# A fused attention, channel-mix and channel-FFN kernel: the planner's ranks from a table, and one temporary in another buffer

## The chip, the cores and the metric

The kernel runs on one core of one Trainium2 chip. The metric is the time of one execution in microseconds of device time (us); lower is better. A core has five engines with an instruction stream each: TensorE (PE, matmuls; PEld are its weight loads), VectorE (DVE), ScalarE (ACT), GpSimd (POOL) and SyncE (SP, which here only issues DMAs). TensorE's clock has two levels, 1.2 and 2.4 GHz; the profile gives the granted share of the full one as PEclk.

## The reference

Three stages follow each other; batch 4, sequence 576, model width 512.

```python
# stage 1: attention, 8 heads of 64; causal window of 32 (heads 0-3), or every 4th of 128 (heads 4-7)
scores = np.where(masks[None], scale * np.matmul(q, k.transpose(0, 1, 3, 2)), -1e9)
attn = np.exp(scores - scores.max(-1, keepdims=True))
x = np.matmul(attn / (attn.sum(-1, keepdims=True) + 1e-9), v)          # -> (4, 576, 512)
# stage 2: channel mix
x_prev = np.concatenate([np.zeros((B, 1, D)), x[:, :-1, :]], axis=1)
xk = mu_k * x + (1.0 - mu_k) * x_prev
xr = mu_r * x + (1.0 - mu_r) * x_prev
k = np.maximum(xk @ w_k, 0.0)                                          # 512 -> 1024
y = 1.0 / (1.0 + np.exp(-(xr @ w_r))) * (k * k @ w_v)                  # r * v
# stage 3: low-rank token mix, then a two-layer FFN over channels
h = y.transpose(0, 2, 1) @ U @ V                                       # rank 32 over the 576 positions
u = y + h.transpose(0, 2, 1)
out = u + np.maximum(u @ w_ch1, 0.0) @ w_ch2                           # 512 -> 2048 -> 512
```

## The kernel before, in words

**The work on TensorE.** The large products run in float32 precision as three matmuls on a high and a low part of each operand: L1006, L1007, L1008 (128x288) in the channel mix, whose positions are cut into 8 chunks of 288 (two for each batch); L1283, L1284, L1285 (128x256) in the FFN's first layer (`ch1`); L1370, L1371, L1372 (128x256) in its second (`ch2`). The FFN's matrix products are saved by a seven-product scheme on 2x2 blocks, so sums and differences of blocks (`ws`, `s`, `tt`, `hb`, `hc`, `ha`) are made on DVE and their high and low parts (`wh`, `wl`, `boxw`, `boxraw`, `boxA`, `boxB`, `boxx`) on ACT, DVE and POOL.

**Between the two.** In the last two chunks of the channel mix the low-rank token mix of batches 0 to 2 runs beside it, that of batch 3 in the FFN's first steps. For each batch: DVE forms `y` = r times v from a PSUM bank (L1100); SP stores it to `ytmp` in DRAM (L1102), and loads a whole batch back as `yb` (L1123, `load_y`, 1152 KB); PE transposes it in five blocks (L1132, `y_tr`), multiplies by U (L1150, `u_mm`, accumulated over the five) and, once ACT and DVE have taken the sum as `g` (L432), by V (L1167, `v_mm`, eight matmuls a batch); DVE adds `yb` (L1175, `us`); SP stores that to `uf` (L1179), from which blocks `ub` of 256 positions come back (L1207) as the FFN's input. `yb` has two buffers. PE executes in the order written, so a `y_tr` whose `yb` has not landed holds up every product behind it.

**What sets the order.** Nothing is issued while the kernel's functions run: each calls `op()`, which appends one of 3453 operations to a list with its engine, an assumed duration and the tiles it reads and writes. `plan()` then orders them. Its `forward(rank)` walks time: for each engine it looks at the operations within WINDOW = 160 of the oldest one not done, sorted by rank (on SP they stay in program order), takes the first that can start, and takes a later one only if that could start more than 100 ns sooner. `backward` works out from such a walk how late each operation may start, plus a bias by kind (EARLIER) and by place (BIAS); a mixture of these over 16 passes is the next rank, first for the first chunks (CUTS), then for the whole. The walk with the earliest end is kept. Where the walk sees PE wait over 600 ns for a PSUM bank's next user (`fill`, L262), it puts matmuls on a tile of zeros ahead of it (L1616, `psS<-zero`, 128x512). The order is then fixed in each engine's instruction stream: on the chip every engine takes its own in turn and waits by semaphore.

**Buffers of the change.** `x_sum(g, name, a, b)` (L1228) makes a difference of two `ub` blocks of group g in a temporary `tt`, which `loose(tag, n, name)` (L568) puts in a slot that another tile used before. Tag "y" has one slot, that of the channel mix's last `y` tiles; tag "m" has one slot, that of the channel mix's mixing temporaries. The FFN runs over five groups of positions, g = 0 to 4; group 0's first step begins while the channel mix ends.

Of the kernel before, what the change touches and what calls it, by code (L numbers as in the profile page):

```python
# [16 lines left out]
B, H, S, D = 4, 8, 576, 64  # L17
DM, DFF, DCH, RANK = 512, 1024, 2048, 32
P = 128
HS = S // 2  # L20
NCH = 2 * B
# [44 lines left out]
BIAS = (-20.0, -20.0, -20.0)  # L66
# [24 lines left out]
PLAN_PRINT = None  # L91
PASSES = 16
CUTS = ((1, 3), (4, 8))
DAMP = 0.8
# [3 lines left out]
EARLIER = {"d": -20, "k2": -10, "wx": -5, "cl": 5}  # L98
# [5 lines left out]
CODE_NS, CODE_BUSY, CODE_GO = 5000.0, 6500.0, 1300.0  # L104


@with_exitstack
def tile_attention_mix_channel(
# [20 lines left out]
    ops, cuts = [], {}  # L129
    bias = 0.0  # L130
# [21 lines left out]
    def op(eng, ns, fn, r=(), w=(), more=100, lock=False, mode=None, size=0):  # L152

        o = Op()
        o.eng, o.ns, o.fn, o.r, o.w, o.more, o.lock, o.mode, o.size = eng, ns, fn, list(r), list(w), more, lock, mode, size
        o.bias = bias
        ops.append(o)

    def plan():
# [30 lines left out]
        def x_end(x):  # L190
            if x.end is not None:
                return x.end
            end = 0.0
            for u in reversed(x.ops):
                if u.i >= upto:
                    continue
                if u.done is None:
                    return NEVER
                end = max(end, u.done)
            x.end = end  # L200
            return end
# [20 lines left out]
        upto = len(ops)  # L222

        def forward(rank):
# [5 lines left out]
            free = dict.fromkeys(("PE", "DVE", "ACT", "POOL", "SP"), 0.0)  # L230
            held = {"DVE": 0.0, "POOL": 0.0}
            queues = {e: [o for o in ops[:upto] if o.eng == e] for e in free}
# [3 lines left out]
            order = []  # L236
# [36 lines left out]
            while len(order) < upto:  # L273
                while ops[low].done is not None:
                    low += 1
                best = None
                for e, q in queues.items():
                    pick = None
                    near = []
# [4 lines left out]
                    if rank and e != "SP":  # L284
                        near.sort(key=lambda o: rank.get(o.i, o.i * 1e6))
                    for o in near:
                        t = ready(o)
                        if t is None:
                            continue
                        t = max(t, free[e])  # L290
                        if o.lock:
                            t = max(t, held["POOL" if e == "DVE" else "DVE"])
                        if o.mode and mode[e] != o.mode:
                            t += 90 if e == "PE" else 1283
                        key = t
# [7 lines left out]
                    if pick and (best is None or pick[0] < best[0]):  # L303
                        best = pick
# [26 lines left out]
            return max(o.done for o in order if o.eng == "PE"), order  # L331

        users = [[] for _ in ops]
        for o in ops:
            for d in o.deps:
                users[d.i].append(o)
            for x in o.first:
                if x.at >= x.bufs:
                    for u in x.line[x.at - x.bufs].ops:
                        if u is not o:  # L340
                            users[u.i].append(o)

        def backward(end, order):

            late = {}
            for o in reversed(order):
                t = end
                for u in users[o.i]:
                    if u.i < upto:
                        t = min(t, late.get(u.i, end) - 40 - (o.done - o.at - o.ns))  # L350
                late[o.i] = t - o.ns
            return {o.i: late[o.i] + 1000.0 * (EARLIER.get(o.kind, 0) + o.bias) for o in order}

        rank = {}
        keep = 0
        for keep_to, upto in [tuple(cuts.get(c, len(ops)) for c in x) for x in CUTS] + [(len(ops), len(ops))]:
            fixed, end = {i: x for i, x in rank.items() if i < keep}, None
            keep = keep_to
            for n in range(PASSES):
                used = dict(rank)  # L360
                got = forward(rank)
                if end is None or got[0] < end:
                    end, best = got[0], used
                    order = [(o, o.at, o.done, o.before) for o in got[1]]
                new = backward(got[0], got[1])
                rank = {i: fixed[i] if i in fixed else DAMP * rank[i] + (1 - DAMP) * x if i in rank else x for i, x in new.items()}
            rank = best if len(best) == upto else rank
            if PLAN_PRINT:
                print("planned to", upto, round(end))
        for o, o.at, o.done, o.before in order:  # L370
            pass
        order = [x[0] for x in order]
# [195 lines left out]
    def loose(tag, n, name):  # L568
        return Part(Lazy([P, n * Q], F32, tag, name, LOOSE[tag]), 0, n * Q)
# [658 lines left out]
    def x_sum(g, name, a, b):  # L1228
        x_slot(g, name)
        t = tt[g, name] = loose("y", 2, "tt")  # L1230
        part_sum(t, a, b, ALU.subtract)
        part_split(T_ENG, t, *operands[g, name])
# [293 lines left out]
    for t in range(NPAIR):  # L1526
        begin(LOADS[t])
        units += fresh(1)
        bias = BIAS[0]
        steps(units[-1:], 2)  # L1530
        bias = 0.0
    for t in range(NPAIR):
        convert_to(t + 1, 1)
        bias = BIAS[1]
        steps(units[t : t + 1], 4)
        mix(0, t, "r")
        bias = BIAS[2]
        first[t]()
        bias = 0.0
# [7 lines left out]
    for c in range(NCH - 1):  # L1547
        cuts[c] = len(ops)
# [28 lines left out]
    cuts[NCH] = len(ops)  # L1577
# [133 lines left out]
```

## Time and profile before

| | |
|---|---|
| time, median of 3 runs | 733.75 us (732.14, 733.75, 734.02) |
| time of the profiled execution | 731.21 us |
| its span, first to last instruction | 729.3 us |
| PE busy | 715.1 us, 98% of the span |
| PE weight loads | 690.8 us, 95% |
| DVE busy | 603.3 us, 83% |
| ACT busy | 420.6 us, 58% |
| POOL busy | 165.2 us, 23% |
| mean granted TensorE clock | 0.995 of full |

The table comes from the page of the profile and from the list of runs. A share of busy time is an average over the whole span: attention and the channel mix to about 345 us, the FFN from there to the end. What an engine waits for in one stretch is read from the waits and the timeline of that stretch. A row of a timeline gives the start and the duration of an instruction; as matmuls are pipelined, the distance from one start to the next is what one costs on PE.

### The profile page before, as it was taken

What the parts mean: (1) busy time and instruction counts of PE and PEld (TensorE: products, weight loads), DVE (VectorE), ACT (ScalarE), POOL (GpSimd) and SP (SyncE); (2) the same over time, 40 slices, a digit from 0 to 9 for tenths busy, and PEclk for the clock granted to TensorE, in tenths of its full rate; (3) what the DMA queues carried; (4) which work ended last, traced back from release to release, by engine and by line L of the source; (5) the groups of instructions that cost most, each with busy time, mean ns of one, the idle gap of its engine ahead of it and who ended that gap; (6) DMA issues with size and microseconds to landing.
All of it is one profiled execution on the core that took longest, in us unless ns stands there. A gap on an engine that the chain in (4) does not pass through costs nothing.

```text
span 729.3 us, 19236 instructions
## 1 busy us (share of the span) xinstructions
PE 715.1 (98%) x7527; PEld 690.8 (95%) x7527; DVE 603.3 (83%) x1500; ACT 420.6 (58%) x1049; POOL 165.2 (23%) x189
## 2 busy tenths in 40 slices
PE   8999999999999999899999999999999999999997
PEld 6778999999999999799899999999999999999997
DVE  5979997889677736599998898999999999797935
ACT  5997867667785837175653543455475545454421
POOL 0101464546463634031200111010000101010100
PEclk9999999999999999999999999999999999999999
DMA  8986268587647520826634456433554111304204
GB/s 314 363 293 216 67 200 284 186 284 250 214 160 255 185 76 26 284 93 204 206 113 169 147 179 208 147 124 116 153 179 131 59 45 56 105 15 133 74 14 130
DMA packets 69963, 117.71 MB, mean 161 GB/s; under 512 B 6128, under 2 KB 41200, under 8 KB 69872
## 3 DMA queue, kind: packets, MB, share of 16 engines
q1 hardware_dynamic: 69872, 116.49, 48.3%
q8 instruction: 59, 0.97, 0.6%
q14 instruction: 32, 0.26, 0.1%
HBM read 85.00 MB, written 31.46 MB: 160 GB/s over the span
## 4 chain that ended last, share of the span: by engine, by line
PE 65%; DVE 17%; issue 7%; DMA 5%; ACT 4%; POOL 1%; SPq 0%; DVEq 0%; POOLq 0%; ACTq 0%
PE psM L1006 7%; PE psM L1008 6%; PE psM L1007 6%; PE psM L1283 6%; PE psM L1285 6%; PE psM L1284 6%; PE psM L1034 4%; PE psS L1372 3%; PE psS L1370 3%; PE psS L1371 3%; PE psM L1370 3%; PE psM L1372 3%; PE psM L1371 3%; DMA w2f<-w 2%; PE psS L923 2%
## 5 line engine op out<-in xcount | busy, mean ns | idle before, releaser
L1006 PE MATMUL psM<-xk,wh 128*128 128x288 f32 x336 | 101.9, 303 | 0.1
L1007 PE MATMUL psM<-xk,wl 128*128 128x288 f32 x336 | 99.5, 296 | 0.0
L1008 PE MATMUL psM<-xk,wh 128*128 128x288 f32 x336 | 99.3, 296 | 0.0
L1006 PE MATMUL psM<-k2s,wh 128*128 128x288 f32 x224 | 67.1, 300 | 0.0
L1007 PE MATMUL psM<-k2s,wl 128*128 128x288 f32 x224 | 66.0, 295 | 0.0
L1008 PE MATMUL psM<-k2s,wh 128*128 128x288 f32 x224 | 65.9, 294 | 0.0
L1006 PEld LDWEIGHTS psM<-xk,wh 128*128 128x128 f32 x336 | 63.6, 189 | 1.2 <-DVE k L1082 0.3
L1007 PEld LDWEIGHTS psM<-xk,wl 128*128 128x128 f32 x336 | 63.7, 189 | 0.2
L1008 PEld LDWEIGHTS psM<-xk,wh 128*128 128x128 f32 x336 | 63.6, 189 | 0.0
L430 POOL TENSOR_TENSOR boxw<-ub,boxw 128x512 fp32r<-128x512 f32 x13 | 19.2, 1475 | 191.7 <-ACT boxw L435 147.8
L430 POOL TENSOR_TENSOR k2s<-k,k2s 128x288 fp32r<-128x288 f32 x49 | 44.3, 908 | 61.8 <-ACT k2s L435 60.6
L1283 PE MATMUL psM<-boxraw,wh 128*128 128x256 f32 x198 | 56.0, 283 | 0.7 <-ACT hc L1353 0.5
L1285 PE MATMUL psM<-boxraw,wh 128*128 128x256 f32 x198 | 55.2, 279 | 0.0
L1284 PE MATMUL psM<-boxraw,wl 128*128 128x256 f32 x198 | 55.1, 279 | 0.0
L1283 PE MATMUL psM<-boxw,wh 128*128 128x256 f32 x186 | 53.6, 288 | 1.3 <-ACT hc L1353 0.7
L1372 PE MATMUL psS<-boxx,wh 128*128 128x256 f32 x192 | 54.3, 283 | 0.0
L1284 PE MATMUL psM<-boxw,wl 128*128 128x256 f32 x186 | 52.3, 281 | 0.0
L1285 PE MATMUL psM<-boxw,wh 128*128 128x256 f32 x186 | 52.2, 281 | 0.0
L722 ACT ACTIVATE pr<-pr,mn 128x64 f32<-128x64 f32 x144 | 48.0, 337 | 6.3 <-DVE mn L713 6.2
L430 POOL TENSOR_TENSOR xk<-m,xk 128x288 fp32r<-128x288 f32 x48 | 42.3, 892 | 34.6 <-ACT xk L435 25.1
L430 POOL TENSOR_TENSOR boxraw<-ub,boxraw 128x512 fp32r<-128x512 f32 x12 | 17.9, 1496 | 125.6 <-ACT boxraw L435 89.2
L435 ACT ACTIVATE boxx<-ha 128x512 fp32r<-128x512 f32 x32 | 20.1, 627 | 41.4 <-DVE ha L591 29.2
(235 smaller groups left out, 2576.8 us busy)
## 6 DMA issues: line engine op xcount, KB each, us to landing
w<-w2raw SPq DMA_DIRECT2D x32, 512.0 KB, 5.3
w<-w1raw SPq DMA_DIRECT2D x20, 512.0 KB, 6.1
w2f<-w SPq DMA_DIRECT2D x32, 256.0 KB, 2.6
ub<-uf SPq DMA_DIRECT2D x32, 256.0 KB, 3.4
ws<-w2f SPq DMA_DIRECT2D x24, 256.0 KB, 3.6
raw<-qk SPq DMA_DIRECT2D x16, 320.0 KB, 6.4
ytmp<-y SPq DMA_DIRECT2D x32, 144.0 KB, 1.9
yb<-ytmp SPq DMA_DIRECT2D x4, 1152.0 KB, 7.1
```

Source lines behind the costliest of these rows:

```text
L430: op("POOL", t, lambda: nc.gpsimd.tensor_tensor(out=out_(), in0=a(), in1=b(), op=ALU.subtract), r, w, 40, lock=True)
L722: nc.scalar.activation(pr[:, d : d + KW], pr[:, d : d + KW], AF.Exp, bias=mn[:, i : i + 1], scale=-1.0, accum_out=sm[:, i : i + 1])
L1006: nc.tensor.matmul(a, lhsT=wh, rhs=xh, start=start, stop=False)
L1007: nc.tensor.matmul(a, lhsT=wl, rhs=xh, start=False, stop=False)
L1008: nc.tensor.matmul(a, lhsT=wh, rhs=xl, start=False, stop=stop)
L1034: pe(2, MM1, lambda o=o, acc=accs[o]: nc.tensor.matmul(acc()[:, :HS], lhsT=whole_w[w]()[:, o * P : (o + 1) * P], rhs=cols(src, n), start=f ...
L1283: nc.tensor.matmul(a, lhsT=wh(*wi), rhs=xh(*ci), start=start and n == 1, stop=False, skip_group_check=True)
L1284: nc.tensor.matmul(a, lhsT=wl(*wi), rhs=xh(*ci), start=False, stop=False, skip_group_check=True)
L1285: nc.tensor.matmul(a, lhsT=wh(*wi), rhs=xl(*ci), start=False, stop=last, skip_group_check=True)
L1370: nc.tensor.matmul(a, lhsT=wh(*wi), rhs=xh(), start=start, stop=False, skip_group_check=True)
L1371: nc.tensor.matmul(a, lhsT=wl(*wi), rhs=xh(), start=False, stop=False, skip_group_check=True)
L1372: nc.tensor.matmul(a, lhsT=wh(*wi), rhs=xl(), start=False, stop=stop, skip_group_check=True)
```

## The change

The ranks no longer come from the passes of `forward` and `backward`: `backward`, the passes and all their constants (BIAS, EARLIER, CUTS, DAMP, PASSES) are gone, and `forward` runs once on `RANKS`, 3453 numbers in steps of 50 ns that are unpacked from a string. The table was found beforehand by a search over shifted ranks, with the mean of five perturbed planner executions as its measure. `forward`, with its windows, assumed durations and fills, is the same; SP's operations still stand in program order among themselves as candidates. In `x_sum`, group 0's `tt` takes the slot of tag "m" and no longer that of "y". The functions of the body are otherwise as before, 54 lines lower; the fill is L1663 and the sorting by rank includes every operation of the list.

```diff
-PASSES = 16
-CUTS = ((1, 3), (4, 8))
-DAMP = 0.8
 NORM_ENG = ("DVE", "DVE", "ACT", "DVE", "POOL")
...
-EARLIER = {"d": -20, "k2": -10, "wx": -5, "cl": 5}
...
+RANKED = (
+    'c-k%73EWrH)(7y@{G`%|kfcExNlJxO<|xs<#t4;^A<8u+xkVx&QOI<OLeivr6^WFRN^^<OK&cd(R66f>y}Lf2)Bc}*)?UMJt-bd6OemUV!#!D{EPLu;p'
...
+)
+RANKS = [50 * x for x in itertools.accumulate(struct.unpack("<3453i", zlib.decompress(base64.b85decode(RANKED))))]
...
-                    if rank and e != "SP":
-                        near.sort(key=lambda o: rank.get(o.i, o.i * 1e6))
+                    if e != "SP":
+                        near.sort(key=lambda o: rank[o.i])
...
-        def backward(end, order):
...
-            return {o.i: late[o.i] + 1000.0 * (EARLIER.get(o.kind, 0) + o.bias) for o in order}
...
-        for keep_to, upto in [tuple(cuts.get(c, len(ops)) for c in x) for x in CUTS] + [(len(ops), len(ops))]:
...
+        order = forward(RANKS)
...
     def x_sum(g, name, a, b):
         x_slot(g, name)
-        t = tt[g, name] = loose("y", 2, "tt")
+        t = tt[g, name] = loose("y" if g else "m", 2, "tt")
         part_sum(t, a, b, ALU.subtract)
         part_split(T_ENG, t, *operands[g, name])
```

Each engine has the same operations as before. Their place in its stream differs for 767 of PE's 945 operations (by 4.6 places in the mean, 35 at most), 905 of DVE's 1175, 503 of ACT's 773, 71 of POOL's 185 and 161 of SP's 375. One fill is new; the others have the sizes they had. Three places follow.

**SP, around the load of batch 1.** `ytmp<-y` stores a tile of the channel mix, `ws<-w2f` loads a block of the second layer's weights, `w2f<-w` stores one, `yb<-ytmp_67` is the load of batch 1. Before:

```order
L1102 DMA ytmp_69<-y 128x288
L621 DMA ws<-w2f_71 128x512
L621 DMA ws<-w2f_70 128x512
L1102 DMA ytmp_69<-y 128x288
L1123 DMA yb<-ytmp_67 128x4x576
L511 DMA w2f_84<-w_4799 128x512
```

and after the change:

```order
L1156 DMA ytmp_69<-y 128x288
L1177 DMA yb<-ytmp_67 128x4x576
L675 DMA ws<-w2f_71 128x512
L675 DMA ws<-w2f_70 128x512
L565 DMA w2f_84<-w_4802 128x512
```

The load of batch 1 has moved up past two loads of weights and one store of `y`. On PE the transposes of batch 1 stand behind 480 products of three matmuls (128x288), where they stood behind 484: twelve matmuls earlier.

**PE, ahead of the transposes of batch 3.** `psS<-vs,g` are the `v_mm` of batch 2; `boxw`, `wh` and `wl` are operands of the FFN's first layer. Before:

```order
L1283 MATMUL psM<-boxw_5407,wh 128x256
L1284 MATMUL psM<-boxw_5407,wl 128x256
L1285 MATMUL psM<-boxw_5407,wh 128x256
L1167 MATMUL psS<-vs,g 128x288 x8
L1283 MATMUL psM<-boxw_5340,wh 128x256
L1284 MATMUL psM<-boxw_5340,wl 128x256
L1285 MATMUL psM<-boxw_5340,wh 128x256
```

(the transposes follow nine matmuls later), and after:

```order
L1337 MATMUL psM<-boxw_5391,wh 128x256
L1338 MATMUL psM<-boxw_5391,wl 128x256
L1339 MATMUL psM<-boxw_5391,wh 128x256
L1221 MATMUL psS<-vs,g 128x288 x4
L1663 MATMUL psS<-zero 128x512 x2
L1186 MATMUL psS<-cst_t,yb 128x128 x4
```

The eight `v_mm` of batch 2 are now in two halves with twelve first-layer matmuls between them (the second half is in the rows), and a fill of two matmuls stands ahead of the transposes of batch 3. In all, 3 `u_mm`, 36 first-layer matmuls and 8 `v_mm` stood between the channel mix's last matmul and those transposes; now 3, 48, 8 and the fill do. From the last `u_mm` to the first `v_mm` there were 12 first-layer matmuls; now there are 24. On SP the load of batch 3 stays behind the last two stores of `y` and one load of `ub`; two more loads of `ub` now stand ahead of those stores. On DVE `tt` of group 0 and the `boxw` made from it stood behind the last `y`; now they stand ahead of the last two.

**PE, the first and second layer's interleaving in an early FFN step.** `boxB,boxA` belong to the second layer, `boxraw` and `boxw` to the first. Before:

```order
L1283 MATMUL psM<-boxw_5340,wh 128x256
L1284 MATMUL psM<-boxw_5340,wl 128x256
L1285 MATMUL psM<-boxw_5340,wh 128x256
L1283 MATMUL psM<-boxraw,wh 128x256
L1284 MATMUL psM<-boxraw,wl 128x256
L1285 MATMUL psM<-boxraw,wh 128x256
```

and after:

```order
L1338 MATMUL psM<-boxw_5345,wl 128x256
L1339 MATMUL psM<-boxw_5345,wh 128x256
L1424 MATMUL psM<-boxB 128x256
L1425 MATMUL psM<-boxB 128x256
L1426 MATMUL psM<-boxB 128x256
L1424 MATMUL psM<-boxB,boxA 128x256
L1425 MATMUL psM<-boxB 128x256
L1426 MATMUL psM<-boxB,boxA 128x256
L1337 MATMUL psM<-boxraw,wh 128x256
```

Six matmuls of the second layer now stand between the product of `boxw` and that of `boxraw`; before, the two followed each other directly. The same six are put between the corresponding products of a later step.

## Rows read from the trace of the kernel before

**Rows 1.** The page: busy us of each engine, share of the span.

```profile
PE 715.1 (98%) x7527; PEld 690.8 (95%) x7527; DVE 603.3 (83%) x1500; ACT 420.6 (58%) x1049; POOL 165.2 (23%) x189
```

**Rows 2.** Waits of PE, whole span: total us, times, longest us.

```profile
PE psS L1132 <- DMA yb<-ytmp: 3.6, 1, 3.6
...
PE psM L1283 <- DVE hb L1333: 0.8, 2, 0.6
```

**Rows 3.** Timeline of PE around the transposes of batch 1.

```profile
299.54 0.29 PE L1008 MATMUL psM<-xk,wh 128*128 128x288 f32 x1
303.40 1.09 PE L1132 MATMUL psS<-cst_t,yb 128*128 128x128 f32 x4 [3.56 <-DMA yb<-ytmp]
...
306.92 0.40 PE L1150 MATMUL psS<-yh,us 128*128 128x512 f32 x1
```

**Rows 4.** Timeline of PE at transposes of batch 0 that did not wait.

```profile
267.01 0.29 PE L1008 MATMUL psM<-xk,wh 128*128 128x288 f32 x1
267.14 0.60 PE L1132 MATMUL psS<-cst_t,yb 128*128 128x128 f32 x4
267.57 0.60 PE L905 MATMUL psS<-cst_t,pr 128*128 128x128 f32 x4
```

**Rows 5.** Windows: PE, PEld, DVE, ACT, POOL busy, PEclk, DMA share, GB/s.

```profile
299.80:303.40 3.60, 0.04 (x2) 0.03 (x1) 0.97 (x3) 0.00 (x0) 0.00 (x0) 0.97 0.98 357
303.40:306.00 2.60, 2.60 (x12) 2.60 (x13) 0.69 (x1) 0.60 (x1) 0.00 (x0) 0.50 0.73 216
```

**Rows 6.** Timeline of SP around the load of batch 1.

```profile
290.46 0.88 SPq L621 DMA_DIRECT2D ws<-w2f  x2
...
292.56 0.53 SPq L1123 DMA_DIRECT2D yb<-ytmp  x1
```

**Rows 7.** DMA issues of 284 to 304 us: KB each, median us to landing.

```profile
yb<-ytmp SPq DMA_DIRECT2D x1, 1152.0 KB, 10.7
...
ytmp<-y SPq DMA_DIRECT2D x4, 144.0 KB, 4.2
ws<-w2f SPq DMA_DIRECT2D x2, 256.0 KB, 3.9
```

**Rows 8.** The tile yb, its four loads, us to landing.

```profile
DMA to landing us min/median/max: 5.9/7.1/10.7
```

**Rows 9.** DMA issues of 348 to 350 us, columns as in rows 7.

```profile
yb<-ytmp SPq DMA_DIRECT2D x1, 1152.0 KB, 5.9
```

**Rows 10.** Timeline of PE, end of the channel mix to batch 3.

```profile
344.82 0.40 PE L1150 MATMUL psS<-yh,us 128*128 128x512 f32 x1
...
345.29 0.28 PE L1283 MATMUL psM<-boxw,wh 128*128 128x256 f32 x1
...
346.70 0.40 PE L1150 MATMUL psS<-yh,us 128*128 128x512 f32 x1
...
349.86 0.80 PE L1167 MATMUL psS<-vs,g 128*128 128x288 f32 x4 [1.34 <-DVE g L432]
...
354.87 0.60 PE L1132 MATMUL psS<-cst_t,yb 128*128 128x128 f32 x4
```

**Rows 11.** Timelines of DVE and SP: the last y, the load of batch 3.

```profile
346.37 0.45 DVE L1100 TENSOR_TENSOR y<-psM,sg 128x288 f32<-128x288 f32 x1
...
349.84 0.69 DVE L591 TENSOR_TENSOR tt<-ub 128x512 f32<-128x512 f32 x1
...
348.70 0.53 SPq L1123 DMA_DIRECT2D yb<-ytmp  x1
```

**Rows 12.** Windows, columns as in rows 5, up to batch 3.

```profile
340.00:350.00 10.00, 8.65 (x66) 8.14 (x65) 9.88 (x21) 5.62 (x11) 0.96 (x1) 1.00 0.40 131
350.00:355.00 5.00, 4.59 (x22) 4.08 (x23) 4.97 (x12) 1.15 (x2) 1.28 (x1) 0.66 1.00 342
```

**Rows 13.** Timeline of PE, an early FFN step and a later one.

```profile
386.38 0.38 PE L1283 MATMUL psM<-boxraw,wh 128*128 128x256 f32 x1 [0.53 <-ACT hc L1353]
...
467.51 0.39 PE L1283 MATMUL psM<-boxw,wh 128*128 128x256 f32 x1 [0.65 <-ACT hc L1353]
```

More of the change, by code (lines that the diff above doesn't have):

```diff
@@ L1 @@
+import base64
+import itertools
+import struct
+import zlib
 from contextlib import ExitStack
@@ L65 @@
 SC_M = 4
-BIAS = (-20.0, -20.0, -20.0)
 LOADS = ("q0 c m w q1", "q2 v1 q3 v0 w", "v2 w", "w w v3 w w w", "")
@@ L126, in f32 @@
         return ap.bitcast(F32)
-    ops, cuts = [], {}
-    bias = 0.0
+    ops = []
     class Lazy:
@@ L155, in op @@
         o.eng, o.ns, o.fn, o.r, o.w, o.more, o.lock, o.mode, o.size = eng, ns, fn, list(r), list(w), more, lock, mode, size
-        o.bias = bias
         ops.append(o)
@@ L194, in x_end @@
             for u in reversed(x.ops):
-                if u.i >= upto:
-                    continue
                 if u.done is None:
@@ L220, in ready @@
             return t
-        upto = len(ops)
         def forward(rank):
@@ L231, in forward @@
             held = {"DVE": 0.0, "POOL": 0.0}
-            queues = {e: [o for o in ops[:upto] if o.eng == e] for e in free}
+            queues = {e: [o for o in ops if o.eng == e] for e in free}
             mode = {"PE": None, "ACT": "exp"}
@@ L272, in fill @@
                 return None, 0, 0
-            while len(order) < upto:
+            while len(order) < len(ops):
                 while ops[low].done is not None:
@@ L330, in forward @@
                 order.append(o)
[L331 to L341, printed above, removed]
-        def backward(end, order):
[L345 to L351, printed above, removed]
-            return {o.i: late[o.i] + 1000.0 * (EARLIER.get(o.kind, 0) + o.bias) for o in order}
-        rank = {}
-        keep = 0
-        for keep_to, upto in [tuple(cuts.get(c, len(ops)) for c in x) for x in CUTS] + [(len(ops), len(ops))]:
[L357 to L372, printed above, removed]
+            return order
+        order = forward(RANKS)
         if PLAN_PRINT:
@@ L1528, in tile_attention_mix_channel @@
         units += fresh(1)
-        bias = BIAS[0]
         steps(units[-1:], 2)
-        bias = 0.0
     for t in range(NPAIR):
         convert_to(t + 1, 1)
-        bias = BIAS[1]
         steps(units[t : t + 1], 4)
         mix(0, t, "r")
-        bias = BIAS[2]
         first[t]()
-        bias = 0.0
     convert_to(NPAIR + 1, 1)
@@ L1547, in tile_attention_mix_channel @@
     for c in range(NCH - 1):
-        cuts[c] = len(ops)
         cur = quanta(c) if c else first
@@ L1576, in tile_attention_mix_channel @@
             prep(*what)
-    cuts[NCH] = len(ops)
     convert_to(len(jobs))
```

94 lines of the change are left out of this document (added).

## The prediction

> **What bounds the kernel now.** I read the page first, then PE's list of waits, then the timelines of the places that the list names, then the windows of clock and DVE there. PE is busy for 715.1 us of a span of 729.3 [rows 1], so all that any order can win is the 14 us in which it is not, and some slow-clock time. DVE with 83% is idle too often to bound the whole, but not in every stretch. The list of waits [rows 2] is short: one wait of 3.6 us for a `yb` load, and then single waits of 1.3 us and less. So three places can pay, and I price each by the distance between starts, which holds slow-clock time as well as idle time.
>
> Place A, the transposes of batch 1: from L1008's start at 299.54 to L1150's at 306.92 [rows 3] PE takes 7.38 us for 13 matmuls of 128x288 and four transposes. At full speed a 128x288 matmul takes 0.13 us (267.01 to 267.14) and four transposes 0.43 (267.14 to 267.57) [rows 4], together 13 x 0.133 + 0.43 = 2.16. So 5.2 us are lost there: about 3.7 in the wait, and 1.5 after it because the granted clock stood at 0.50, the 1.2 GHz level, for the 2.6 us that followed it [rows 5].
>
> Place B, from the channel mix's last matmul to the transposes of batch 3: 344.82 to 354.87 is 10.05 us [rows 10] for 3 `u_mm` at 0.235 (two from 344.82 to 345.29), 36 first-layer matmuls at 0.118 (twelve in the 1.41 us from 345.29 to 346.70) and 8 `v_mm` at 0.133: 0.7 + 4.2 + 1.1 = 6.0. So 4.05 are lost: 1.34 waiting for `g`, the rest in a shorter wait behind it and to a clock that averaged 0.66 from 350 to 355 [rows 12]. DVE is full there, 14.85 of 15 us from 340 to 355 [rows 12]. The batch 3 transposes themselves did not wait: the load was issued at 348.70 [rows 11], 2.3 us after the start of the last `y` at 346.37, and took 5.9 [rows 9], which makes 354.6, just before PE came at 354.87.
>
> Place C: two first-layer products wait 0.53 and 0.65 us for ACT to read their bank into `hc` [rows 13].
>
> **The change part by part.** No operation goes; the work on each engine is the same, so only waits and clock can change.
>
> A. The load of batch 1 now stands where the two `ws` loads were issued, at 290.46 in place of 292.56 [rows 6]: 2.1 us earlier. PE comes to its transposes twelve matmuls earlier, at 299.7 - 1.6 = about 298.1. What decides is how long the load takes. It took 10.7 us, the longest of four; the shortest took 5.9, and the median is 7.1 [rows 8]. From 290.46 these make 301.2 (10.7), 296.4 (5.9) and 297.6 (7.1). I take 7.1: the 656 KB that went out just ahead of it (two `ws` of 256 and a `ytmp` of 144, [rows 7]) are now behind it, and the load of batch 3, with two `ytmp` and one `ub` ahead, took 5.9 [rows 9]; but the 656 KB still run beside it. Then PE does not stop, the clock stays up, and all 5.2 us come back. Bounds: -0.6 (10.7 again: PE still waits from 298.1 to 301.2, 3.1 us, and the 1.5 of clock stay: 5.2 - 3.1 - 1.5 = 0.6) and -5.2. The `ws` loads and the store that now come behind are 2 us later; the first `ws` consumers are the DVE sums of the FFN's weights, ahead of which DVE had half its time free (0.97 of 3.6 us busy, [rows 5]).
>
> The rows leave open how far the load runs beside its neighbours: the `ws` loads of this stretch took 3.9 us and the `ytmp` stores 4.2 in the median [rows 7], and 357 GB/s were moved while PE waited [rows 5]. If only what is ahead of it counted, it would land at 292.56 + 10.7 = 303.3 less the 1.9 us that 656 KB take at 357 GB/s, so at 301.4: 3.3 us of wait left, a gain of 0.4 in place of 5.2. The Trainium skill (DMA: Bandwidth & Descriptors, "Queues, rings and completion order") speaks for this: SP owns one ring on each DMA engine, and an engine consumes its descriptors in ring order, so a transfer issued later would not take bandwidth from one issued earlier. By that rule A would be -0.4 and the time 733.1 in place of 728.3. I keep it as R1; the 5.9 of batch 3 [rows 9] says that a load with little ahead is quick, and at 290.46 less is ahead than at 292.56.
>
> B. Twelve more first-layer matmuls (1.4 us) fit ahead of the transposes of batch 3, and the wait for `g` gets 24 matmuls of cover (2.8 us) where it had 12: its 1.34 us go, and the shorter one with it, for the second half of the `v_mm` stands behind twelve more. But the chain `y`, store, load that ends in `yb` stays: PE comes after 0.7 + 48 x 0.118 + 1.1 = 7.4, with the fill (two matmuls of 512 columns at 0.23) 7.9 us, and the load, if it lands as late after the last channel-mix matmul as before, at 10.0. So a wait of about 2 us for `yb` takes the place of that for `g`, and the clock falls after it as it did at A, up to 1.5 us. The interval remains 10.05 us long, holds 1.4 us more work, and pays up to 1.5 behind it: zero. Bounds: -1.5 (the clock stays up) and +1.5 (two more `ub` loads of 256 KB stand ahead in SP's queue, 512 KB at 357 GB/s = 1.5 us later).
>
> The moved buffer belongs here: in slot "m" `tt` need not wait until the last `y` tiles are stored, and its matmuls are half of the new cover. On DVE it and its `boxw`, 1.4 us as two instructions of 0.7 (`tt` took 0.69 [rows 11]), now come ahead of the last two `y`. I cost that at nothing, because other DVE work for the weights moves behind the `y` in exchange; without that, on a full DVE, the last `y` and with it the load are 1.4 us later, which the bound of +1.5 covers.
>
> C. Six second-layer matmuls, 6 x 0.118 = 0.71 us, now lie between the products at both places: more than 0.53 and 0.65, so both waits go: -1.2 (bounds -1.2 and 0). The two waits for `hb` [rows 2] have the same matmuls ahead as before and stay.
>
> D. The rest of the new order. 767 of PE's operations have moved, and each step of the FFN could meet a wait of the size that such waits have now, about half a microsecond (0.53 and 0.65 [rows 13], 0.8 in two [rows 2]). I take two of 0.5, +1.0 (bounds 0 and +2.5, five of them).
>
> Sum: 731.2 (the profiled execution) - 5.2 + 0 - 1.2 + 1.0 = 725.8. That execution was 2.5 us below the median of its three runs, 733.75, so on the footing of the median the forecast is 725.8 + 2.5 = **728.3 us**, 0.7% less. About 0.3%, 2.2 us, is what a measurement of this kernel can tell from no change: faster is below 731.5, slower above 736.0.
>
> **The rivals.**
>
> R1, the load of batch 1 lands late all the same. For it: 357 GB/s were moving while PE waited [rows 5], so bytes may be what the load waits for, and the weights that stood ahead still share the DMA engines when they are behind. By the Trainium skill's rule on ring order (DMA: Bandwidth & Descriptors, same section) it is this rival that comes true. Against it: half of the four loads took 7.1 us or less. A gives 0.4 to 0.6, so 731.2 - 0.6 - 1.2 + 1.0 + 2.5 = 732.9, or 733.1: within 0.3%.
>
> R2, DVE gives back at B what A wins. For it: DVE has 14.85 of 15 us filled up to 355 [rows 12], so if it was behind by its own work and not by PE's, the last `y` comes no earlier, and PE, 5.2 us ahead, waits for `yb` as much longer. Against it: DVE was free for much of 299.8 to 306 [rows 5], so the work that follows PE moves forward with it. Then 731.2 - 1.2 + 1.0 + 2.5 = 733.5: no change.
>
> R3, slower: the first- and second-layer steps stall in the new order. Two waits for ACT's read into `hc` now hold PE up, at 0.59 us each [rows 13]. The place is the FFN from 355 us on, the mechanism that a product reaches its bank before ACT has read it. From the forecast to 736.0 it takes 7.7 us, 13 such waits; with 14 of them the time is 736.6. For it: the order is fixed by assumed durations, and two waits show that these are off by half a microsecond in places. Against it: the changed order puts six matmuls where the two worst were.
>
> **How the numbers follow.** The forecast has a chance of 0.60, R1 0.12, R2 0.16, R3 0.12. The forecast is all faster, R1 and R2 lie within 0.3% (a small part of R1 with a good B is faster), R3 is slower: faster 0.61, same 0.27, slower 0.12. The range: its lower end is the best case, A -5.2, B -1.5, C -1.2, D 0, 723.3 on the profiled execution's footing and 725.8 on the median's; I set 724.5 between them. The upper end is to hold R1 and most of R2: 733.6. The likeliest case alone would have 725 to 731.
>
> **What would show it.** In the changed kernel's trace: the load of batch 1 issued near 290.5 and landing by 298, with no wait of PE for `yb` at its transposes and the clock at the 2.4 GHz level through 300 to 306 (A); a wait for `yb` of about 2 us at batch 3, none for `g`, and a stretch at 1.2 GHz behind it (B); no wait for `hc` at the two places of rows 13 (C); the list of waits otherwise with a few entries of half a microsecond (D). The prediction is wrong if `yb` still holds PE up at batch 1 for 3 us (R1), if the wait at batch 3 grows to 5 us and more (R2), or if the list of waits shows a dozen waits for `hc` or `hb` in the FFN (R3).

## The result: 725.3 us in place of 731.9, and the profile after

The changed kernel takes **725.26 us**, the median of 6 executions (723.6 to 726.49); the kernel before, on the same chips, 731.93 (6 executions, 730.68 to 734.02). The ratio is 0.9904, 95% interval 0.9882 to 0.9925: faster by about 1%. The forecast was a ratio of 728.3 / 733.75 = 0.9926, just above the upper end of that interval. In microseconds it was 3.0 too high; 1.8 of that is the baseline, whose three runs then known had a median of 733.75, where all six have 731.93. The profiled execution took 726.0 us (span 724.2), where the forecast on that footing was 725.8.

The page, busy us of each engine, answers to [rows 1]: PE is busy for as long within 1 us, and the span is 5.1 us shorter, so most of what went is time in which PE stood.

```profile
PE 714.3 (99%) x7529; PEld 689.3 (95%) x7529; DVE 593.0 (82%) x1500; ACT 424.1 (59%) x1049; POOL 164.5 (23%) x189
```

Waits of PE in the changed kernel, columns as in [rows 2]:

```profile
PE psM L1337 <- DVE hb L1387: 1.2, 2, 0.6
PE psS L1186 <- DMA yb<-ytmp: 0.9, 1, 0.9
PE psS L1663 <- DVE us L1229: 0.5, 1, 0.5
...
PE psS L1221 <- DVE g L486: 0.4, 2, 0.2
...
PE psM L1337 <- ACT hp L1362: 0.4, 1, 0.4
```

The 3.6 us for `yb` are gone, and so is `hc`; `g` is down from 1.3 to 0.4 in two waits. The two for `hb` have grown from 0.8 [rows 2] to 1.2. A wait of 0.9 for `yb` is new, and it is that of batch 3.

**Place A in the changed kernel.** SP issues the load of batch 1 ahead of the `ws` loads; the DMA issues of 290 to 290.6 us (KB, us to landing) give 6.0 us for it, and PE's timeline runs through the transposes:

```profile
290.15 0.53 SPq L1177 DMA_DIRECT2D yb<-ytmp  x1
290.78 1.04 SPq L675 DMA_DIRECT2D ws<-w2f  x2
```

```profile
yb<-ytmp SPq DMA_DIRECT2D x1, 1152.0 KB, 6.0
```

```profile
297.62 0.60 PE L1186 MATMUL psS<-cst_t,yb 128*128 128x128 f32 x4
297.97 0.38 PE L1060 MATMUL psM<-xk,wh 128*128 128x288 f32 x1
```

The load landed at 290.15 + 6.0 = 296.15 and PE came 1.5 us later, with no wait in brackets. The windows (columns as in [rows 5]) show the clock at its full level where it had been at 0.50:

```profile
299.80:303.40 3.60, 3.60 (x29) 3.34 (x28) 3.49 (x9) 0.93 (x2) 0.00 (x0) 1.00 0.82 282
303.40:306.00 2.60, 2.60 (x21) 2.51 (x20) 1.46 (x4) 0.16 (x1) 0.00 (x0) 1.00 0.61 185
```

**Place B in the changed kernel**, PE from the end of the channel mix (339.86 is the `u_mm` that stood at 344.82 in [rows 10]) to the transposes of batch 3 and what follows them:

```profile
339.86 0.40 PE L1204 MATMUL psS<-yh,us 128*128 128x512 f32 x1
...
345.15 0.80 PE L1221 MATMUL psS<-vs,g 128*128 128x288 f32 x4 [0.24 <-DVE g L486]
...
347.50 1.50 PE L1221 MATMUL psS<-vs,g 128*128 128x288 f32 x4
...
349.52 0.73 PE L1663 MATMUL psS<-zero 128*128 128x512 f32 x2 [0.53 <-DVE us L1229]
351.20 1.11 PE L1186 MATMUL psS<-cst_t,yb 128*128 128x128 f32 x4 [0.94 <-DMA yb<-ytmp]
352.68 0.58 PE L1337 MATMUL psM<-boxw,wh 128*128 128x256 f32 x1 [0.37 <-ACT hp L1362]
...
355.20 0.41 PE L1339 MATMUL psM<-boxw,wh 128*128 128x256 f32 x1
```

```profile
351.19:358.01 6.82, 6.44 (x27) 5.75 (x28) 2.89 (x7) 4.33 (x9) 0.00 (x0) 0.50 0.51 169
```

The transposes come 11.34 us after that `u_mm`, where it was 10.05. Behind them the matmuls start 0.21 us apart (353.06 to 355.20 is ten of them), and the window shows why: for 6.8 us the granted clock is 0.50, the 1.2 GHz level. In the trace of before the matmuls behind these transposes started 0.12 apart:

```profile
355.55 0.28 PE L1285 MATMUL psM<-boxw,wh 128*128 128x256 f32 x1
355.67 0.28 PE L1283 MATMUL psM<-boxw,wh 128*128 128x256 f32 x1
```

Why `yb` is late stands on DVE and SP and in the DMA issues of 341.5 to 345.9 us:

```profile
341.38 0.46 DVE L1154 TENSOR_TENSOR y<-psM,sg 128x288 f32<-128x288 f32 x1
```

```profile
340.33 1.86 SPq L1156 DMA_DIRECT2D ytmp<-y  x2
...
345.40 0.53 SPq L1177 DMA_DIRECT2D yb<-ytmp  x1
```

```profile
q1 hardware_dynamic: 502, 0.49, 38.7%
q8 instruction: 1, 0.02, 2.2%
...
yb<-ytmp SPq DMA_DIRECT2D x1, 1152.0 KB, 5.8
...
ytmp<-y SPq DMA_DIRECT2D x1, 144.0 KB, 3.5
```

The last `y` starts 1.52 us after the `u_mm`, as before (346.37 less 344.82 is 1.55), and the load takes 5.8, as before. But the load is issued 4.02 us after that `y`, where it was 2.33 [rows 11]: the store between them took 3.5 us to land, where it had taken 1.7 (below, from the DMA issues of 346.5 to 349.2 us before). One load of 16 KB on queue q8, of the kind that the profile calls "instruction", runs beside it.

```profile
ytmp<-y SPq DMA_DIRECT2D x1, 144.0 KB, 1.7
```

**Where the time went.** To set all kernels side by side I worked out the time that PE loses: the distance from each PE instruction's start to the next, less the median distance in that run for its line of the kernel, summed over a stretch. A is 68 instructions around the transposes of batch 1; B goes from the channel mix's last matmul to 30 instructions past the transposes of batch 3. Each row is one profile. Sums over the two long stretches depend on what counts as alike: with one median per matmul shape, the same for both kernels, what changes behind B is -3.6 us where the table has -4.0.

| us lost by PE | A | B | B to 400 us | 400 us to the end |
|---|---|---|---|---|
| before | 5.16 | 4.07 | 2.94 | 3.35 |
| changed | 0.11 | 6.77 | 1.57 | 0.69 |
| changed, second profile (a1) | 0.18 | 6.99 | 2.26 | 0.96 |
| e1, e6: before, load of batch 1 early | 1.80, 1.06 | 3.95, 3.78 | 2.96, 2.88 | 3.14, 3.15 |
| e2: changed, that load late | 5.84 | 6.91 | 1.78 | 0.68 |
| e3: changed, buffer as before | 0.19 | 5.13 | 5.23 | 0.36 |
| e5: changed, `ub` loads behind | 0.16 | 9.69 | 1.87 | 1.05 |
| e7, e10: changed, longer first fill | 0.18, 0.23 | 2.69, 3.40 | 1.65, 1.72 | 1.38, 0.63 |
| e12, e13: the same, fill at B out | 0.20, 0.10 | 6.18, 5.45 | 1.31, 1.71 | 0.41, 0.30 |
| e8: changed, waits for `hc` back | 0.20 | 5.55 | 1.86 | 1.42 |

Changed less before: A -5.05; B +2.70, and the two matmuls of the fill, 0.47, which count as work, +3.2 in all; behind B -4.0, of which the two waits for `hc` are 1.5 by starts; between A and B +0.6. Together -5.3, and the span is 5.1 shorter. Starts alone, without medians, say it more plainly: the `u_mm` at the end of the channel mix comes 4.96 us earlier (339.86 for 344.82), and from it to the end of the span it takes 384.4 us as before, 0.1 less.

### The profile page after: what moved, and what is told of

It is laid out like the page before. It is cut to its first block, busy times and chain, and to the rows that moved or that the text cites. A ratio compares the mean times of both kernels' runs of the same rounds, so it can differ in the third digit from the quotient of the medians.

```text
span 724.2 us, 19254 instructions
## 1 busy us (share of the span) xinstructions
PE 714.3 (99%) x7529; PEld 689.3 (95%) x7529; DVE 593.0 (82%) x1500; ACT 424.1 (59%) x1049; POOL 164.5 (23%) x189
## 5 line engine op out<-in xcount | busy, mean ns | idle before, releaser
L484 POOL TENSOR_TENSOR xk<-m,xk 128x288 fp32r<-128x288 f32 x48 | 44.0, 927 | 32.7 <-ACT xk L489 27.6
```

The source lines that it names most:

```text
L484: op("POOL", t, lambda: nc.gpsimd.tensor_tensor(out=out_(), in0=a(), in1=b(), op=ALU.subtract), r, w, 40, lock=True)
```

## The experiments

Each is an edit to the fixed order or to a fill. `moved(order, [(i, j)])` takes operation i out of the planned order and puts it ahead of operation j; nothing else moves. Medians are over 6 to 12 executions, ratios to the kernel before on the same chip (medians 731.6 to 731.8 us).

### The load of batch 1, alone in each order: e1, e2

e1 is the kernel before with only the load of batch 1 moved, past the two `ws` loads and the store; e2 is the changed kernel with that load put back behind two `ws` loads and a `w2f` store.

```diff
+        order = moved(order, [(1376, 1471)])   # e1, in before
+        order = moved(forward(RANKS), [(1376, 1366)])   # e2, in the changed kernel
```

> The kernel before with one DMA moved: SP issues the load of batch 1 ahead of the two ws loads and the ytmp store that stood right before it; every other engine's stream is that of before. First theory (the load's place in SP's queue is the greater part of the gain): issued near 290.5 us, landing near 296.5, no wait of PE for yb at the transposes of batch 1, clock at the upper level from 300 to 306, the stretch from 299.5 to 306.9 shorter by 5.2 us; time 0.6 to 0.7% under before (ratio 0.993). Rival (the gain comes from the new order as a whole, and this load is bound by bytes): landing at 301 or later, PE waits at least 1.5 us, ratio 0.998 to 1.000. Second rival (DVE gives it back at the end of the channel mix): the wait goes at batch 1 but the time from the last channel-mix matmul to the transposes of batch 3 grows from 10.0 to about 15 us.

> The changed kernel with the load of batch 1 put back behind two ws loads and one w2f store in SP's queue; PE's stream is unchanged. First theory: the load goes out 2 to 3 us later, lands at 300 or later, PE, which comes at 297.6, waits 2 to 4 us for yb and runs at the lower clock level for some 2.5 us after it: 3.5 to 5.5 us over the changed kernel, ratio to before 0.995 to 0.998. Rival (the new order as a whole brings the gain): under 1.5 us over the changed kernel, ratio 0.990 to 0.992.

Measured: e1 728.84, ratio 0.9968 (0.9946 to 0.9990); e2 731.44, 0.9990 (0.9971 to 1.0010). So undoing this one move leaves no gain that can be told from none, and doing it alone gives about a third of the gain by the ratios (2.8 us by the medians). In e2 the wait is there again:

```profile
303.31 1.09 PE L1186 MATMUL psS<-cst_t,yb 128*128 128x128 f32 x4 [4.40 <-DMA yb<-ytmp]
```

```profile
293.56 0.53 SPq L1177 DMA_DIRECT2D yb<-ytmp  x1
```

The tile `yb` in e2 gives the time of the four loads; the slowest is this one, so it landed at 293.56 + 9.6 = 303.2:

```profile
DMA to landing us min/median/max: 5.6/7.2/9.6
```

It went out 2.69 us after the store of `y` ahead of it (290.87), in the changed kernel 0.41 (289.74 to 290.15), so 2.3 us later in its place, and was 3.6 slower in flight; PE loses 5.84 us there. The rest of e2's row in the table is the changed kernel's: what the new order loses at B it has won behind B, and no more.

In e1 the load did what it was to do, 5.8 us, but PE met another wait four microseconds later. Timelines of PE and of DVE in e1:

```profile
302.30 0.60 PE L1132 MATMUL psS<-cst_t,yb 128*128 128x128 f32 x4
...
306.31 0.51 PE L1150 MATMUL psS<-yl,us 128*128 128x512 f32 x1 [1.57 <-DVE yl L432]
```

```profile
302.61 0.42 DVE L591 TENSOR_TENSOR s<-ws 128x256 f32<-128x256 f32 x1 [2.06 <-DMA ws<-w2f]
```

The DMA issues of 294 to 297 us in e1:

```profile
yb<-ytmp SPq DMA_DIRECT2D x1, 1152.0 KB, 5.8
ws<-w2f SPq DMA_DIRECT2D x2, 256.0 KB, 7.0
```

The `ws` loads, now behind 1152 KB, took 7.0 us. DVE stood 2.06 us for them at a sum that PE did not need yet, and `yl`, which PE needed at once, was queued behind that sum. A therefore kept 1.80 of its 5.16 us. The changed kernel's DVE waits there too, 1.21 us at 298.28, but in its order nothing of PE's path is behind.

### Is it DVE's order that costs e1 its gain? e6

```diff
+        order = moved(order, [(1376, 1471), (1473, 1368), (1474, 1368), (1475, 1368)])   # before, three sums of ws behind yl
```

> The kernel before with the load of batch 1 ahead of the two ws loads, as in the first experiment, and with the three DVE sums that read these ws (s, ws, s) put behind yl of batch 1's first block. Theory (the first experiment gained less than the 5.2 us of place A because DVE stood 2.06 us before such a sum, its ws landing 7 us after issue, and yl queued behind it held PE up for 1.6 us): no wait of PE for yl near 306 us, place A costs nothing, 1.5 to 2 us under the first experiment, ratio to before 0.993 to 0.995. Rival (the rest of the gain sits elsewhere): the yl wait goes and another takes its place, ratio 0.996 to 0.998 as before.

Measured: 728.87, 0.9961 (0.9941 to 0.9981). The wait for `yl` fell to 0.8 us and A to 1.06, so the chain is the right one, but half of it remains (the waits of 295 to 312 us):

```profile
PE psS L1150 <- DVE yl L432: 0.8, 1, 0.8
```

The time is e1's within either interval; 0.7 us cannot be told by it.

### The two waits for hc: e8, and e9, which told nothing

e8 is the changed kernel with the six second-layer matmuls taken out from between the two products at both places; e9 is e1 with such matmuls put between them.

```diff
+        order = moved(forward(RANKS), [(1780, 1765), (2202, 2175), (2200, 2175), (2203, 2175)])   # e8
+        order = moved(order, [(1376, 1471), (1765, 1780), (2175, 2202)])   # e9, in before
```

> The changed kernel with the six second-layer matmuls taken out again from between the two products at both places of rows 13, so that these follow each other as in the kernel before. First theory (the six matmuls cover ACT's read into hc): waits of PE for hc of 0.5 to 0.7 us at both places are back, 1.2 to 1.5 us over the changed kernel. Rival (these waits are made up by later slack): the time of the changed kernel.

> The kernel before with the load of batch 1 moved as in the first experiment, and with six second-layer matmuls put between the two first-layer products at the two places where PE waited for hc, as in the changed kernel. First theory (two places explain the gain, the rest of the new order costs as much as it brings): 5.2 + 1.2 = 6.4 us under before, ratio 0.991, equal to that of the changed kernel; no wait for hc in the list of PE's waits. Rival (the rest of the new order matters): ratio 0.993 or more, the hc waits reappear as waits for other tiles.

Measured: e8 725.74, 0.9917 (0.9887 to 0.9948), 0.4 us over a1 and so not to be told from it. Its waits of 360 to 480 us have the two entries back:

```profile
PE psM L1337 <- ACT hc L1407: 1.1, 2, 0.5
```

That the order removes these waits is shown; that they are worth 1.2 us is not contradicted, and not shown by the time. In e9 (729.77, 0.9977 with 0.9959 to 0.9996) both moved products were issued ahead of DVE's read of the bank that they overwrite, so two `hb` tiles hold other numbers and PE's waits there (1.7 us for `hc`) belong to another chain: inconclusive.

### The buffer without which these ranks gain nothing: e3

```diff
-        t = tt[g, name] = loose("y" if g else "m", 2, "tt")
+        t = tt[g, name] = loose("y", 2, "tt")
```

> The changed kernel with the temporary tt of group 0 back in the slot of tag y, and the planner's one walk over the same ranks: tt then has to wait for the last y, so the order from the end of the channel mix on differs from that of the changed kernel in many places. First theory (the moved buffer lets 24 first-layer matmuls cover g; without it PE waits for g again): a wait of PE of 1 us or more for g or boxw at the end of the channel mix, 0 to 2 us over the changed kernel. Rival (the walk finds other work to put there): within 0.5 us of the changed kernel; third possibility: the instruction load falls elsewhere and batch 3 comes sooner, up to 3 us under it.

Measured: 731.15, 1.0006 (0.9984 to 1.0027). The planner walks the same ranks, but `tt` must wait for the last stores of `y`, and from the end of the channel mix on the order comes out differently. PE's waits in e3:

```profile
PE psS L1204 <- DVE yl L486: 2.3, 3, 1.6
PE psM L1337 <- DVE hb L1387: 2.2, 2, 1.3
PE psS L1221 <- DVE g L486: 2.0, 1, 2.0
...
PE psS L1221 <- DVE us L1229: 1.4, 1, 1.4
```

The wait for `g` is back, and 5.23 us are lost between B and 400 us. No table searched with the old buffer was run, so ranks and buffer cannot be priced apart.

### What makes the store at B late: e5, e7, a1

Two theories for the store of 3.5 us: the two further `ub` loads that stand ahead of it in SP's queue, or the instruction load beside it. e5 puts three `ub` loads behind the load of batch 3. e7 makes the fill at the kernel's start of 28 matmuls of 128 columns in place of 7 of 512, 42 more instructions with their weight loads, and touches nothing else: it shifts the moments at which the instruction loads fall. a1 is the changed kernel again, for e7's chip.

```diff
+        order = moved(forward(RANKS), [(1669, 1538), (1670, 1538), (1667, 1538)])   # e5
-            for _ in range(many):   # e7
+            for _ in range(28 if many == 7 else many):
...
```

> The changed kernel with three loads of ub moved behind the load of batch 3 in SP's queue. First theory (what holds up batch 3 is the store of the last y, which lands 3.5 us after its issue because loads of ub share the DMA engines with it): that store lands in about 1.8 us, the load of batch 3 goes out near 343.7 in place of 345.4 and lands near 349.5, no wait of PE for yb is left at its transposes, 1 to 3 us under the changed kernel, ratio to before 0.986 to 0.989. Rival (DVE's us, and not the load, sets the pace there): the load lands earlier, but PE comes to the transposes no more than 1 us sooner and the clock falls all the same; within 1 us of the changed kernel.

> The changed kernel with the first fill of zeros written as 28 matmuls of 128 columns in place of 7 of 512: the same columns, but 42 more PE instructions (weight loads counted), so that PE's instruction loads of 16 KB, which come once in so many instructions, come some 2.5 us earlier everywhere after. Theory (the last store of y takes 3.5 us and not 1.7 because an instruction load at 342.5 us, 1.5 us long, holds one of the 16 DMA engines that carry it): that store lands in 1.7 to 2.1 us, the load of batch 3 goes out near 343.7 in place of 345.4, no wait of PE for yb at batch 3 is left, 1 to 3 us under the changed kernel. Rival (the store is slow for another reason, or the collision only moves to another transfer): the store still takes over 3 us, or the load of batch 3 takes 7 us and more; within 1 us of the changed kernel.

> The changed kernel as it is, so that the others of this set have it beside them on the same chip: ratio to before 0.988 to 0.993.

Measured: e5 729.66, 0.9981 (0.9958 to 1.0003); e7 727.22, 0.9938 (0.9916 to 0.9960); a1 725.33, 0.9912 (0.9881 to 0.9942). With the `ub` loads gone from ahead of it the store still took 3.5 us in e5, and the instruction load still ran (DMA issues of 341.5 to 346 us):

```profile
q8 instruction: 1, 0.02, 1.3%
...
ytmp<-y SPq DMA_DIRECT2D x1, 144.0 KB, 3.5
```

So the first theory falls. The `ub` that now come late hold ACT up for 7.26 us, and through it PE by 3.32; with it B loses 2.9 us more than in the changed kernel, most of the 4.3 by which the median is higher:

```profile
354.14 0.63 ACT L489 ACTIVATE boxraw<-ub 128x512 fp32r<-128x512 f32 x1 [7.26 <-DMA ub<-uf]
```

```profile
355.82 0.58 PE L1337 MATMUL psM<-boxw,wh 128*128 128x256 f32 x1 [3.32 <-ACT hp L1362]
```

In e7 no 16 KB load falls on the store, which takes 1.7 us again (DMA issues of 346.1 to 350.6 us), and PE finds `yb` there:

```profile
q1 hardware_dynamic: 596, 0.65, 56.9%
...
ytmp<-y SPq DMA_DIRECT2D x1, 144.0 KB, 1.7
```

```profile
354.14 0.73 PE L1663 MATMUL psS<-zero 128*128 128x512 f32 x2 [0.53 <-DVE us L1229]
354.71 0.60 PE L1186 MATMUL psS<-cst_t,yb 128*128 128x128 f32 x4
```

B falls from 6.77 to 2.69 us. The time does not follow, since the start takes it back: the new fill took 6.24 us in place of 3.35, the next one 2.07 in place of 1.20, and by the transposes of batch 1 PE was 4.7 us later than in the changed kernel.

### The same shift without its price, and the fill at B: e10, e12, e13

e10 fills with 4 matmuls of 512 columns and 24 of 32x32, the same count of instructions; e12 also leaves out the fill ahead of the transposes of batch 3; e13 also puts three of DVE's weight operations behind the `us` sums.

```diff
-            for _ in range(many):
+            for k in [0] * 4 + [32] * 24 if many == 7 else [0] * many:   # e10, e12, e13
...
+            onto, wide, many = o.i != 1656 and getattr(o, "before", None) or (None, 0, 0)   # e12, e13
+        order = moved(forward(RANKS), [(1631, 1644), (1623, 1644), (1643, 1644)])   # e13
```

> The changed kernel with 42 more PE instructions in its first fill as in the code-shift experiment, but at no time of its own: 4 zero matmuls of 512 columns and 24 of 32, in place of 7 of 512 (in the code-shift experiment 28 matmuls of 128 columns took 6.2 us in place of 3.3, which hid what was won). Theory (the instruction load that collides with the last store of y costs about 4 us at batch 3): that store lands in 1.7 to 2.1 us, no wait of PE for yb at batch 3, from the last channel-mix matmul on 3 to 4 us shorter; time 3 to 4 us under the changed kernel, ratio to before 0.985 to 0.988. Rival (what was won there is lost at the start or at another collision): ratio 0.990 to 0.992.

> The same with the changed kernel's new fill ahead of the transposes of batch 3 (two zero matmuls) left out. First theory (with the load of batch 3 on time the fill only costs its own 0.47 us): 0 to 0.5 us under the run with the fill, the clock stays at its upper level. Rival (the fill keeps the clock up): a stretch at the lower level after the transposes, 1 us or more over the run with the fill.

> The same as the last (shift, no fill) with three DVE instructions for weights (s, wl, s) put behind the eight us of batch 2, which they stood ahead of. Theory (what is left at batch 3 is PE's wait for banks that us frees, and DVE comes to us 1.5 us late): the eight v_mm take 1 us less, 0.5 to 1.5 us under the last run. Rival (DVE is full there, and what is put behind is late for PE instead): no change, or a wait of PE for wl or boxB.

Measured: e10 724.4, 0.9905 (0.9872 to 0.9937); e12 724.53, 0.9894 (0.9860 to 0.9928); e13 726.18, 0.9921 (0.9891 to 0.9951). The store took 2.6, 1.9 and 1.8 us, no transposes of batch 3 waited for `yb`, and in e10 the clock stayed at its full level:

```profile
352.00:355.00 3.00, 2.72 (x21) 2.58 (x22) 2.25 (x5) 3.00 (x7) 0.00 (x0) 1.00 0.75 231
```

Without the fill it fell in the same place (e12), though PE's wait there was of similar length, 0.86 us for `us` against 0.54 ahead of e10's fill:

```profile
353.00:356.00 3.00, 2.91 (x13) 2.91 (x14) 2.26 (x5) 3.00 (x7) 0.00 (x0) 0.50 0.79 237
```

In e13 PE waits 3.30 us for `us`: moving those weight operations did not help. The profiled execution of e10 has a span of 721.4 us, 2.8 less than the changed kernel's; its median is only 0.9 below a1's, inside the intervals, where 3 to 4 were expected. A reason that fits: the fall at B does not come in every execution. The 6.8 us at half clock of the profile make by themselves a mean of 0.995 over the span. The mean granted clock of the changed kernel's 13 executions (a1's among them) was 0.994 or 0.995 in eight, with a median of 725.75 us, and 0.998 to 1.0 in five, with 724.31, as much as e10; of e10's six executions five had 0.999 or 1.0, of e12's, without the fill, one. Where the clock fell in executions that were not profiled is not shown. So none of these versions is shown to beat the changed kernel.

## Why the prediction was right, and where two of its terms were not

The sum came out (725.8 forecast, 726.0 measured) and the net gain sits where it was put. That it came out so closely is luck: two terms were off by about 3 us with opposite signs.

**A, right**: -5.05 measured, -5.2 forecast. The load was issued at 290.15 (forecast 290.5) and took 6.0 us (7.1 taken). e2 shows that without the move no net gain is left. The sentence under it, that the later `ws` loads are covered because DVE had half its time free, was wrong as a reason: e1 shows DVE standing 2.06 us for them, with `yl` behind. A free share is no cover on an engine that works in order; what saved the changed kernel is that its order has nothing urgent behind that wait. In the order of before, the same move is worth 3.4 us at A. And the 1.5 us of slow clock in A are those of one execution: of 75 of the kernel before, run beside the experiments, 43 had a mean granted clock of 0.995 or less (median 732.5 us) and 23 one of 0.998 or more (730.7).

**R1, refuted.** It had the load land late for the bytes beside it; it landed in 6.0 us with the two `ws` loads issued right behind it. The Trainium skill's rule (DMA: Bandwidth & Descriptors, "Queues, rings and completion order"), that an engine takes descriptors in ring order, is not what failed: the load landed at 296.15 and the `ws` loads issued after it held DVE until 298.28. What failed is the price that I worked out beside it, 1.9 us for 656 KB at 357 GB/s. With 768 KB ahead, the load of e2 took 9.6 us, 3.6 more than with them behind, where 768 KB at 357 GB/s are 2.2.

**B, mis-sized**: forecast 0 with bounds of 1.5 either way, measured +3.2. The wait for `g` went as forecast (0.24 in place of 1.34), and the last `y` came as early after the channel mix as before, so R2 did not come true. The reading of before that B rested on was wrong in one part: e1 has the order of before at B and a clock of 1.00 there, and lost 3.95 us where before, with its slow stretch, lost 4.07. PE waited for DVE instead, 0.7 us for `boxw` among it, so the slow clock cost the kernel before next to nothing at this place (a window of e1, columns as in [rows 5]):

```profile
349.00:354.00 5.00, 3.75 (x20) 2.78 (x21) 4.94 (x13) 1.15 (x2) 1.29 (x1) 1.00 0.91 316
```

In the changed kernel two parts came out larger than forecast. The load of batch 3 was issued 1.7 us later after that `y`, because its store took 3.5 us; the wait for `yb` at 0.94 us is shorter than the 2 forecast because `us` and the fill had already made PE late. And the slow clock cost more than the 1.5 us that I took from A: it lasted from 351.2 to 358.0 us. Ahead of the transposes PE lost 11.34 less the 7.9 of work forecast there, 3.4 us; the rest of the 6.77, 3.3 us, was lost behind them, where before it lost nothing (4.05 of its 4.07 lay ahead). Not all of the 3.4 is the load's: in e7, where `yb` was there in time, the transposes came 10.23 us after the `u_mm`, so 1.1 goes with the late load and 2.3 are left with DVE's `g` and `us`. The bound of +1.5 priced bytes of `ub`, which e5 shows to be no part of it. e7 and e10 show that with the instruction load elsewhere the wait for `yb` is gone; in their profiles the clock holds too.

**C, as forecast in the trace**: no wait for `hc` is left at the two places, 1.1 to 1.5 us by e8's and before's rows. The time could not tell it.

**D, wrong sign**: forecast +1.0 (0 to +2.5), measured about -2: behind B PE lost 4.0 us less, 1.5 of it being C; by the second profile the gain without C is 1.6. R3 is refuted with it: the list of waits has no new one for `hb` or `hc`, and the two for `hb` grew by 0.4 in all. From 400 us on the steps of PE that took 0.2 to 0.4 us, where 0.118 is the usual, fell from 17 to 5, and the mean distance of matmuls from 119.3 ns (2,724 in 325 us) to 118.5 (2,701 in 320), by the windows below (before, then changed; columns as in [rows 5]). The prediction took those short holds as a property of such orders and only counted new ones. Which operation each of them waited for was not separated.

```profile
400.00:725.00 325.00, 324.15 (x2724) 323.07 (x2723) 282.80 (x555) 156.75 (x304) 28.90 (x19) 1.00 0.36 112
```

```profile
400.00:720.00 320.00, 319.37 (x2701) 318.95 (x2700) 280.71 (x552) 156.27 (x303) 26.28 (x19) 1.00 0.36 112
```

So e2's result has a plain reading: without A, the new order's gain in the FFN and its loss at B cancel.

## What to carry to other kernels

Where a DMA's landing holds up the busiest engine, look first at its place in the issuing queue: here that was worth as much as all else in an order of which hundreds of operations had moved. But follow what it overtakes to the engine that waits for that, and look at what stands behind that wait, since idle time there is no cover. A stall on TensorE is to be priced with the slow-clock stretch that follows it, which can be longer than the stall, and only where PE is not held by another engine in that stretch. And when a chain of store and load comes out late for no reason in the order, look in the list of DMA queues for what else ran in those microseconds.

## What was not expected of the hardware

The last 144 KB store of `y` took 3.2 to 3.5 us in the five profiles (changed, a1, e2, e5, e8) in which one 16 KB load of the "instruction" queue q8 began beside it, and 1.7 to 2.6 in those of before, e1, e3, e7, e9, e10, e12 and e13, in which none did (8 KB loads of q14, of the same kind, ran beside it in e7, e10 and e12; of e6 the trace lacks the landing). In e5's single packets 120 of the store's 128 packets of 1152 bytes had run by 343.17 us; the instruction load ran from 343.13 for 0.93 us, and the last eight, as many as one of 16 DMA engines has of 128, came only when it ended, from 344.05 to 344.82. That those eight and the load had the same engine is a reading of these times; the trace does not name the engine. The Trainium skill (DMA: Bandwidth & Descriptors, "Queues, rings and completion order") says that an engine turns from one queue to the next only at the end of a packet; the trace has this load as one record, with which that agrees. And 42 more PE instructions at the start moved that load by 5.6 to 6.7 us against the end of the channel mix (e7, e10, e12, e13): an edit far away decided whether a transfer here was late.
